# Clustered attention feeding a dense mixture of experts: values' sums on TensorE, scales kept in PSUM, a sign step on ScalarE, three pairs' marks written in place, new ranks in the plan

## The chip, the core and the metric

The kernel runs on one core of a Trainium2 chip. The metric is the device time of one execution in microseconds (us), as the median of several runs. Engines are named as in the profile: PE is TensorE's matmul, PEld its weight load, DVE is VectorE, ACT is ScalarE, POOL is GpSimd, and SP is the queue that issues the DMAs.

## The reference, cut to what matters

```python
def _attn_ref(q, k, v, centroids):                  # q, k, v: (4, 8, 768, 64)
    scale = 1.0 / np.sqrt(D)
    q_assign = np.argmax(np.einsum('bhsd,hcd->bhsc', q_n, c_n), axis=-1)   # 16 clusters
    k_assign = np.argmax(np.einsum('bhsd,hcd->bhsc', k_n, c_n), axis=-1)
    mask = q_assign[:, :, :, None] == k_assign[:, :, None, :]
    scores = np.where(mask, scale * np.matmul(q, k.transpose(0, 1, 3, 2)), -1000000000.0)
    scores = scores - np.max(scores, axis=-1, keepdims=True)
    attn = np.exp(scores)
    attn = attn / (np.sum(attn, axis=-1, keepdims=True) + 1e-09)
    return np.matmul(attn, v)

def _moe_ref(x, w_gate, w1, w2):                    # x: (3072, 512), 8 experts of 1024
    P = np.exp(logits - logits.max())               # logits = x @ w_gate
    ...                                             # 8 rounds: P scaled by its row sums, then its column sums
    for e in range(E):
        out += P[:, e:e + 1] * (np.maximum(x @ w1[e], 0.0) @ w2[e])
```

A query whose cluster has no key at all gets the plain mean of the values: all its scores are equal.

## The kernel before

The program has two stages, each laid out by a planner that is part of the kernel. The first is the attention of 32 heads, in 16 pairs; the second, which starts on PE some 496 us into the execution, is the mixture of experts. Only the attention stage is touched.

**A pair of heads.** `load_pair` brings a pair's q and k in. `scale_pair` takes their sums of squares on ACT (L633), adds them up over the partitions with a product with ones (L639), and works two powers of two out of them on DVE (L642 to L652). `split_pair` writes each operand as a half-precision part and a rest (ACT L666, DVE L668). The parts are transposed: for the first `EARLY` pairs by PE and a copy (`turn`, L698 and L700), for the others by a DMA (L682). `assign_pair` finds the cluster of every row (PE L739 and L750, five DVE steps L756 to L766, PE L778) and puts the clusters as marks into extra rows of the operands `X`: for pair 0 straight out of PSUM (DVE L788, ACT L791), for every other pair by way of a tile `ot` (ACT L802) and four DMAs (L810).

**A head.** `max_chunk` computes scores of 512 columns on PE (L834) and takes their row maximum on DVE (L838), nine chunks a head. `max_rows` turns the maxima into two more rows of the operand (L881, L883, L892). `exp_chunk` computes the scores again with the maxima taken off (PE L930 and L931), takes the exponential on ACT (L937) and adds it up on POOL (L959). `values` multiplies with v on PE in full precision (L995), three times a pair; `norm` divides.

**A group of four heads.** `load_group` loads v and prepares the mean of the values for rows without keys. On DVE two reductions add the six blocks of v (L593, two heads each), one product with ones adds the partitions up (PE L597), a DVE step scales and masks it (`ms`, L600), ACT rounds it (`mh`, L604), and DVE multiplies that with a sign (`mh2`, L608) and adds the rest (`ve`, L611). There are eight groups.

**What sets the order.** Each step is a generator that yields the engine and an estimated duration, and the planner takes the step that can start first, with small rank numbers first among those close together. Instructions then run on each engine in the planned order. Buffers are handed out by `Tokens`: `t_x` stands for the two PSUM tiles named `misc_ps`, which the scales, the clusters, the rows, the group sums and the norms all share. A generator that waits for one gets it by its rank. `"DVE*"` and `POOL` in the plan stand for steps that the planner doesn't lay beside each other.

Of the kernel before, what the change touches and what calls it, by code (L numbers as in the profile page):

```python
# [42 lines left out]
class Tokens:  # L43


    def __init__(self, n):
        self.times, self.waiters = [0.0] * n, []

    def put(self, plan):
        self.times.append(plan.now.time + plan.LATENCY)  # L50
        if self.waiters:
            w = min(self.waiters, key=lambda w: w.key)
            self.waiters.remove(w)
            w.time = max(w.time, self.times.pop())
            plan.resumed.append(w)


class Process:
    def __init__(self, gen, key, time):
        self.gen, self.key, self.time, self.options, self.value, self.engine = gen, key, time, (), None, None  # L60


class Planner:
# [36 lines left out]
    def advance(self, w):  # L100

        while True:
            self.now = w
            try:
                r = w.gen.send(w.value)
            except StopIteration:
                return
            w.value = None
            if isinstance(r, float):
                w.time += r  # L110
            elif isinstance(r, Event):
                if r.time is None:
                    r.waiters.append(w)
                    return
                w.time = max(w.time, r.time)
            elif isinstance(r, Tokens):
                if not r.times:
                    r.waiters.append(w)
                    return
                r.times.sort()  # L120
                w.time = max(w.time, r.times.pop(0))
            else:
# [7 lines left out]
    def run(self):  # L130
        while True:
            while self.resumed:
                self.resumed.sort(key=lambda w: w.key)
                self.advance(self.resumed.pop(0))
# [3 lines left out]
            for i, w in enumerate(self.ready):  # L138
                for o in w.options:
                    engine = o[0].rstrip("*/:")  # L140
                    start = max(w.time + self.latency(w.engine, engine), self.free.get(engine, 0.0))
                    if len(o) == 4:
                        start = max(start, self.loaded + o[2])
                    if o[0] in self.PORT:
                        start = max(start, self.port)
                    if engine == "PE" and o[0][2:] != self.mode:
                        start += 0.1
                    steps.append((start, start + (o[2] if len(o) == 3 else 0.0), w.key, i, w, o, engine))
            first = min(steps, key=lambda x: x[1:4])
# [23 lines left out]
def attn_moe_kernel(  # L173
# [176 lines left out]
    with ExitStack() as actx:  # L350
# [68 lines left out]
        assert 8 * C == P  # L419
        om_scale = const.tile([P, 1], F32, name="om_scale")  # L420
        om_bias = const.tile([P, 1], F32, name="om_bias")
        for h in range(2):
            for t, one, other in ((om_scale, MARK, MARK), (om_bias, 0.0, -MARK)):
                nc.vector.memset(t[4 * h * C : (4 * h + 2) * C, :], one)
                nc.vector.memset(t[(4 * h + 2) * C : 4 * (h + 1) * C, :], other)

# [48 lines left out]

        EARLY = 2
        KEYS = dict(load=-20, split0=-98.0, split1=-72.5, split2=-33.5, assign=-49.0, place=-50.0, chain=-47.5, ones=-49, turn=-40, max=-27, rows=-38.0, exp=0, values=13.5, out=12.0, batch=27.0, group=-30.0, vsplit=-17.0, vsum=-10, group0=-18.5, inputs=8, first=1000)
# [67 lines left out]
        ev = Events()  # L545
        t_x, t_s, t_m, t_v = Tokens(2), Tokens(2), Tokens(2), Tokens(1)
        t_nat, t_sc, t_pe, t_nh, t_vn = Tokens(2), Tokens(1), Tokens(PB), Tokens(6), Tokens(2)
# [21 lines left out]
        def load_group(n):  # L569
            b, g = n // H, n % H // G  # L570
            hs = slice(g * G, (g + 1) * G)
            if True:
                yield ev["x", 0, 1, "k"]
            if n >= G:
                yield ev["e", 0]
            yield t_vn
            t = groups[(b, g)] = {}
            yield SP, 0.625
            vn = vals.tile([P, G, NT, D], F32, name="vn")
            nc.sync.dma_start(  # L580
                out=vn.rearrange("p h t d -> p h (t d)"), in_=v[b, hs].rearrange("h (p t) d -> p h (t d)", t=NT)
            )
            yield plan.copied(3.2) - plan.now.time

            plan.now.key = urgency("vsum", n)
            yield t_mean
            vsum = None
            for i in range(2):
                yield DVE, 0.9
                if i == 0:  # L590
                    vsum = nat.tile([P, G, D], F32, name="vsum", bufs=1)
                hh = slice(i * G // 2, (i + 1) * G // 2)
                nc.vector.tensor_reduce(out=vsum[:, hh], in_=vn[:, hh].rearrange("p h t d -> p h d t"), axis=AX, op=ALU.add)  # L593
            yield t_x
            yield PE, 0.64, 0.107, 0.213
            ps = misc_tile()
            nc.tensor.matmul(ps[:, 0 : G * D], ones, vsum.rearrange("p h d -> p (h d)"), start=True, stop=True)  # L597
            yield DVE, 0.4
            ms = sm.tile([4, G * D], F32, name="ms", bufs=1)
            nc.vector.tensor_tensor(out=ms, in0=ps[0:4, 0 : G * D], in1=halves.rearrange("p h d -> p (h d)"), op=ALU.mult)  # L600
            t_x.put(plan)
            yield ACT, 0.4
            mh = sm.tile([4, G * D], F32R, name="mh", bufs=1)
            nc.scalar.copy(mh, ms)  # L604
            yield ev["cleared"]
            yield "DVE*", 0.45
            mh2 = sm.tile([4, G * D], F32, name="mh2", bufs=1)
            nc.vector.tensor_scalar(out=mh2, in0=mh.bitcast(F32), scalar1=sgn4, scalar2=None, op0=ALU.mult)  # L608
            yield "DVE*", 0.4
            ve = ves[n // G % 2]  # L610
            nc.vector.scalar_tensor_tensor(  # L611
                out=ve[0:4].rearrange("p h d -> p (h d)"), in0=ms, scalar=odd, in1=mh2, op0=ALU.mult, op1=ALU.add
            )
            t_mean.put(plan)
            t.update(vn=vn, ve=ve)
            ev["group", b, g].set(plan)
# [7 lines left out]
        def scale_pair(p):  # L624
# [14 lines left out]
            nc.tensor.matmul(ps[:, 0:2], ones, ss, start=True, stop=True)  # L639
            yield DVE, 0.16  # L640
            g = sm.tile([P, 2], F32, name="sg")
            nc.vector.tensor_scalar(out=g, in0=ps[:, 0:2], scalar1=32.0, scalar2=None, op0=ALU.max)  # L642
            t_x.put(plan)
            yield DVE, 0.6
            nc.vector.tensor_scalar(
# [77 lines left out]
        def assign_pair(p):  # L723
# [55 lines left out]
            plan.now.key = urgency("ones", 2 * p)  # L779
            if p == 0:  # L780
                for x in range(2):
                    for h in range(2):
                        for j, w in enumerate("qk"):
# [5 lines left out]
                            else:  # L789
                                yield ACT, 0.48  # L790
                                nc.scalar.activation(to, psb[rows, 0:HS], AF.Identity, scale=om_scale[rows, :], bias=om_bias[rows, :])  # L791
                    for w in "qk":
                        ev["x", 0, x, w].set(plan)
                t_x.put(plan)
                t_sc.put(plan)
                return
            for h in range(2):
                yield ACT, 0.369
                if h == 0:
                    ot = nat.tile([4 * C, S], F16, name="ot", bufs=1)  # L800
                rows = slice(h * 4 * C, (h + 1) * 4 * C)
                nc.scalar.activation(  # L802
                    ot[:, h * HS : (h + 1) * HS], psb[rows, 0:HS], AF.Identity, scale=om_scale[rows, :], bias=om_bias[rows, :]
                )
# [14 lines left out]
        def max_chunk(n, c):  # L819
# [12 lines left out]
            for y in range(ni):  # L832
# [3 lines left out]
                )  # L836
            yield DVE, 0.598
            nc.vector.tensor_reduce(  # L838
# [76 lines left out]
        def exp_chunk(n, c):  # L915
# [18 lines left out]
            yield t_pe  # L934
            yield ACT, 0.5
            pe = t["pe", c] = work.tile([P, ni, z - a], F32, name="pe", bufs=PB)
# [33 lines left out]
        def values(p):  # L970
# [12 lines left out]
            av = None  # L983
            for u in range(NCH // 3):
                for c in range(3 * u, 3 * u + 3):
                    for x in range(2):
                        yield ev["p", n + x, c]
                yield "PE:", 2.8, 0.107, 0.43
                if u == 0:
                    av = ps_v.tile([P, 1024], F32, name="av_ps")  # L990
                for c in range(3 * u, 3 * u + 3):
                    i0, ni, a, z = CHUNKS[c]
# [922 lines left out]
```

## Time and profile before

| | us |
|---|---|
| median of 3 runs | 2298.12 |
| lowest and highest | 2297.12, 2299.38 |
| the profiled execution | 2296.4 |
| its span, first to last instruction | 2294.5 |
| first product of the second stage on PE | 496 |

The profile is of one execution. For each engine it gives the busy time, for each group of instructions the count and mean duration, and what ended the idle time before them. A view named the chain of waits follows the work that ended last back from the last instruction, from each step to what released it; a piece of it is time that nothing else covered, by that reading. PE's records overlap one another because matmuls are pipelined, so a PE that is busy all the time by its records is not at its peak.

### The profile page before, as it was taken

To read this page: it belongs to the slowest core of one execution; us is meant where nothing else is said; L and a number is where in the kernel's file an instruction comes from. 1 tells how busy PE (TensorE), PEld (TensorE's weight loads), DVE (VectorE), ACT (ScalarE), POOL (GpSimd) and SP (SyncE) were. 2 spreads that over 40 slices of the span, in tenths; PEclk is the share of its full clock that TensorE was granted. 3 is DMA by queue.
4 is the path that set the end of the run, shared out by engine and by line. 5 is a ranking of instruction groups with operands and counts; after the bars stand their busy time and mean duration, and the time that the engine had idled before them with its cause. 6 is when DMAs were issued, how large, how long until landed. Compare 5 with 4: busy or idle time off the path is not lost.

```text
span 2294.5 us, 43172 instructions
## 1 busy us (share of the span) xinstructions
PE 2204.4 (96%) x16218; PEld 1531.3 (67%) x16218; DVE 1886.6 (82%) x3627; ACT 1199.4 (52%) x2318; POOL 1379.0 (60%) x1361
## 2 busy tenths in 40 slices
PE   5899999988989999999999999999999999999998
PEld 2344444445767777777777777777777777777777
DVE  7888988869977987788779877987897789777776
ACT  6577766666555545454535453545454444545432
POOL 5477777979755756464737473747465655556431
PEclk7899999999999999999999999999999999999999
DMA  4556543434522524163426232523343253414242
GB/s 121 125 128 168 133 115 102 134 123 157 194 90 74 180 79 141 58 189 88 142 63 199 70 115 86 170 78 107 122 136 112 72 164 95 134 49 135 61 138 78
DMA packets 176235, 271.00 MB, mean 118 GB/s; under 512 B 59429, under 2 KB 108825, under 8 KB 175513
## 3 DMA queue, kind: packets, MB, share of 16 engines
q1 hardware_dynamic: 176024, 268.24, 39.2%
q8 instruction: 127, 2.08, 0.4%
q14 instruction: 84, 0.68, 0.1%
HBM read 225.82 MB, written 23.69 MB: 109 GB/s over the span
## 4 chain that ended last, share of the span: by engine, by line
PE 82%; DVE 10%; ACT 2%; issue 2%; DMA 2%; POOL 1%; SPq 0%; DVEq 0%; ACTq 0%; POOLq 0%
PE a_ps L1604 21%; PE a_ps L1788 14%; PE ac_ps L1788 12%; PE c_ps L1788 11%; PE c_ps L1604 10%; PE b_ps L1604 5%; PE av_ps L995 3%; DVE mrt L838 3%; PE exp_ps L930 2%; PE max_ps L834 2%; PE exp_ps L931 1%; ACT pe L937 1%; DVE k L668 1%; POOL psum L959 1%; DVE xT L1090 0%
## 5 line engine op out<-in xcount | busy, mean ns | idle before, releaser
L1788 PEld LDWEIGHTS <-h 128*128 128x128 f16 x8064 | 790.1, 98 | 193.3 <-issue 8.1
L1604 PEld LDWEIGHTS <-wa 128*128 128x128 f16 x5376 | 526.6, 98 | 272.7 <-issue 14.5
L1644 POOL TENSOR_TENSOR h<-s,h 128x384 f16<-128x384 f32 x127 | 125.1, 985 | 540.0 <-ACT h L1642 522.9
L1633 ACT ACTIVATE h<-c 128x384 f16<-128x384 f32 x384 | 200.5, 522 | 437.2 <-DVE c L1627 435.7
L1788 PE MATMUL a_ps<-wb,h 128*128 128x256 f16 x3072 | 377.2, 273 | 0.7 <-DVE acc L1828 0.6
L1788 PE MATMUL ac_ps<-wb,h 128*128 128x256 f16 x2688 | 366.6, 273 | 1.4 <-DVE acc L1824 1.4
L1788 PE MATMUL c_ps<-wb,h 128*128 128x256 f16 x2304 | 285.1, 274 | 4.0 <-DVE acc L1824 2.8
L1828 DVE SCALAR_TENSOR_TENSOR acc<-a_ps,gates,acc 128x256 f32<-128x256 f32 x460 | 215.2, 479 | 89.4 <-PE a_ps L1788 86.8
L959 POOL TENSOR_TENSOR psum<-psum,pe 128x256 f32<-128x256 f32 (+1 forms) x240 | 249.5, 1066 | 44.1 <-ACT pe L937 41.2
L1644 POOL TENSOR_TENSOR h<-c,h 128x384 f16<-128x384 f32 x252 | 249.9, 1004 | 23.9 <-ACT h L1642 22.7
L1635 DVE SCALAR_TENSOR_TENSOR h<-c,h 128x384 f16<-128x384 f32 x384 | 254.7, 666 | 6.9 <-ACT h L1633 6.7
L937 ACT ACTIVATE pe<-exp_ps,escs 128x512 f32<-128x512 f32 x288 | 189.8, 683 | 58.2 <-PE exp_ps L931 52.0
L1828 DVE SCALAR_TENSOR_TENSOR acc<-ac_ps,gates,acc 128x256 f32<-128x256 f32 x402 | 192.3, 478 | 33.5 <-PE ac_ps L1788 31.3
L838 DVE TENSOR_REDUCE mrt<-max_ps 128x1 f32<-128x512 f32 (+1 forms) x288 | 189.3, 681 | 36.3 <-PE max_ps L834 34.6
L1828 DVE SCALAR_TENSOR_TENSOR acc<-c_ps,gates,acc 128x256 f32<-128x256 f32 x344 | 155.8, 477 | 74.8 <-PE c_ps L1788 74.3
L1624 ACT ACTIVATE c<-a_ps 128x384 f32<-128x384 f32 x256 | 125.1, 489 | 161.3 <-PE a_ps L1604 159.9
L1642 ACT CAST h<-c 128x384 f16<-128x384 f32 x256 | 128.3, 509 | 83.0 <-DVE c L1718 82.8
L1644 POOL TENSOR_TENSOR h<-h,h 128x384 f16<-128x384 f32 x124 | 139.9, 1128 | 36.0 <-PE c_ps L1788 23.9
L930 PE MATMUL exp_ps<-T 128*128 128x512 f16 (+1 forms) x384 | 125.4, 339 | 9.5 <-ACT pe L937 8.9
L834 PE MATMUL max_ps<-X 96*128 96x256 f16 (+1 forms) x384 | 110.0, 344 | 24.6 <-DVE mrt L838 20.6
L995 PE MATMUL av_ps<-pe,vn 128*64 128x512 f32 (+1 forms) x768 | 133.1, 491 | 0.0
L931 PE MATMUL exp_ps<-X 98*128 98x512 f16 (+1 forms) x384 | 125.5, 339 | 0.9 <-ACT X L865 0.9
(497 smaller groups left out, 3710.7 us busy)
## 6 DMA issues: line engine op xcount, KB each, us to landing
raw<-in_moe_w SPq DMA_DIRECT2D x120, 512.0 KB
qn<-in_q SPq DMA_DIRECT2D x16, 384.0 KB
kn<-in_k SPq DMA_DIRECT2D x16, 384.0 KB
vn<-in_v SPq DMA_DIRECT2D x8, 768.0 KB
xd<-xT SPq DMA_DIRECT2D x4, 1536.0 KB
xqB<-xd SPq DMA_DIRECT2D x16, 384.0 KB
out<-acc SPq DMA_DIRECT2D x16, 384.0 KB
X<-T SPq DMA_DIRECT2D x60, 96.0 KB
```

The lines of the kernel that those rows point to most:

```text
L834: nc.tensor.matmul(ps[:, y * (z - a) : (y + 1) * (z - a)], t["qa"][0:96, i * P : (i + 1) * P], t["k2"][0:96, a:z], start=True, stop=True)
L838: nc.vector.tensor_reduce(out=t["mr"][:, i0 : i0 + ni, ni - 1], in_=ps.rearrange("p (x c) -> p x c", x=ni), axis=AX, op=ALU.max)
L930: nc.tensor.matmul(o, t["k1"][:, ki], t["q1"][:, a:z], start=True, stop=False)
L937: nc.scalar.activation(pe, ps.rearrange("p (x c) -> p x c", x=ni), AF.Exp, scale=pairs[p]["exp"])
L959: (nc.gpsimd if w == POOL else nc.vector).tensor_tensor(out=st[:, a:z], in0=old[a], in1=part, op=ALU.add)
L995: nc.tensor.matmul(av[o, a:z], vn[:, i, :], heads[t]["pe", c][:, i - i0], start=(i == 0), stop=False, skip_group_check=True)
L1604: nc.tensor.matmul(ps[:, 0:HB], wt[:, w_, a, c, :], xv[:, x_, c, :], start=(n in (0, 1, 5) and s_ == 0), stop=(s_ == len(steps) - 1), skip ...
L1633: nc.scalar.activation(t[:, 0], c, AF.Relu)
L1635: nc.vector.scalar_tensor_tensor(out=t[:, 1], in0=c, scalar=0.0, in1=t[:, 0], op0=ALU.max, op1=ALU.subtract)
L1644: by(w).tensor_tensor(out=t[:, 1], in0=c, in1=t[:, 0], op=ALU.subtract)
L1788: nc.tensor.matmul(view(m, i), t[:, a_, i * P : (i + 1) * P], w[:, b_, x, :], start=(opens and n == 0 and i in (0, 2)), stop=(n == 5), ski ...
L1828: nc.vector.scalar_tensor_tensor(out=to, in0=src, scalar=gate[b, e][:, ti : ti + 1], in1=to, op0=ALU.mult, op1=ALU.add)
```

## The change

- **Group sums.** The two DVE reductions are gone; six products of ones with the six blocks of v accumulate in one PSUM tile. The planner's estimate for this step on PE goes from 0.64 to 0.85.
- **Sign step.** ACT writes `mh` already multiplied with the sign (`scale=sgn4`), and the DVE step of `mh2` is gone.
- **Scales.** The four intermediate steps on DVE work in place in the PSUM tile that the product left, and the tile is given back after the fifth instead of after the first.
- **Three early pairs.** `EARLY` is 3 instead of 2, and the first three pairs' marks are written straight from PSUM (DVE and ACT), as pair 0's were. A constant `MARK` replaces the tile `om_scale`.
- **Ranks.** Holding a `t_x` token lifts a generator's rank by 30 until it gives the token back. Two estimates grow (0.598 to 0.66, 0.5 to 0.6). `VU` is 3, which is what stood there.

```diff
-    def __init__(self, n):
-        self.times, self.waiters = [0.0] * n, []
+    def __init__(self, n, lift=0.0):
+        self.times, self.waiters, self.lift = [0.0] * n, [], lift
     def put(self, plan):
+        plan.now.lift -= self.lift
...
-            w = min(self.waiters, key=lambda w: w.key)
+            w = min(self.waiters, key=lambda w: w.key - w.lift)
...
+            w.lift += self.lift
...
-                    steps.append((start, start + (o[2] if len(o) == 3 else 0.0), w.key, i, w, o, engine))
+                    steps.append((start, start + (o[2] if len(o) == 3 else 0.0), w.key - w.lift, i, w, o, engine))
...
-        EARLY = 2
+        EARLY, LIFT, VU = 3, 30.0, 3
...
-        t_x, t_s, t_m, t_v = Tokens(2), Tokens(2), Tokens(2), Tokens(1)
+        t_x, t_s, t_m, t_v = Tokens(2, LIFT), Tokens(2), Tokens(2), Tokens(1)
...
             yield t_mean
-            vsum = None
-            for i in range(2):
-                yield DVE, 0.9
...
-                nc.vector.tensor_reduce(out=vsum[:, hh], in_=vn[:, hh].rearrange("p h t d -> p h d t"), axis=AX, op=ALU.add)
             yield t_x
-            yield PE, 0.64, 0.107, 0.213
+            yield PE, 0.85, 0.107, 0.12
             ps = misc_tile()
-            nc.tensor.matmul(ps[:, 0 : G * D], ones, vsum.rearrange("p h d -> p (h d)"), start=True, stop=True)
+            for i in range(NT):
+                nc.tensor.matmul(ps[:, 0 : G * D], ones, vn[:, :, i, :], start=(i == 0), stop=(i == NT - 1))
...
-            nc.scalar.copy(mh, ms)
+            nc.scalar.activation(mh, ms, AF.Copy, scale=sgn4)
             yield ev["cleared"]
-            yield "DVE*", 0.45
-            mh2 = sm.tile([4, G * D], F32, name="mh2", bufs=1)
-            nc.vector.tensor_scalar(out=mh2, in0=mh.bitcast(F32), scalar1=sgn4, scalar2=None, op0=ALU.mult)
...
-            yield DVE, 0.16
-            g = sm.tile([P, 2], F32, name="sg")
-            nc.vector.tensor_scalar(out=g, in0=ps[:, 0:2], scalar1=32.0, scalar2=None, op0=ALU.max)
-            t_x.put(plan)
-            yield DVE, 0.6
+            yield DVE, 0.8
+            g = ps[:, 0:2]
+            nc.vector.tensor_scalar(out=g, in0=g, scalar1=32.0, scalar2=None, op0=ALU.max)
...
             nc.vector.tensor_scalar(out=es, in0=g[:, 0:1], scalar1=g[:, 1:2], scalar2=SCALE, op0=ALU.mult, op1=ALU.mult)
+            t_x.put(plan)
...
-            if p == 0:
+            if p < EARLY:
...
-                                nc.scalar.activation(to, psb[rows, 0:HS], AF.Identity, scale=om_scale[rows, :], bias=om_bias[rows, :])
+                                nc.scalar.activation(to, psb[rows, 0:HS], AF.Identity, scale=MARK, bias=om_bias[rows, :])
```

The plan of the whole attention stage comes out differently. Two places follow.

PE, right after the first head's rows (`av_ps`) are transposed; `T_185` and `X_186` are head 0's operands, `X_188` head 1's. Before:

```order
L863 MATMUL av_ps<-ident,mr_547 6x128
L930 LDWEIGHTS T_185
L930 MATMUL exp_ps<-T_185 128x512
L931 LDWEIGHTS X_186
L931 MATMUL exp_ps<-X_186 128x512
```

And now:

```order
L855 MATMUL av_ps<-ident,mr_532 6x128
L593 MATMUL misc_ps<-vn,ones 128x256 x6
L826 LDWEIGHTS X_188
L826 MATMUL max_ps<-X_188 128x512
L922 LDWEIGHTS T_185
L922 MATMUL exp_ps<-T_185 128x512
```

The first group's six products, and scores of head 1 for its maxima, now stand ahead of the first scores for an exponential; the group's one product stood some seventy rows further down before.

DVE, where the scales of pair 2 are worked out. Before:

```order
L642 TENSOR_SCALAR sg<-misc_ps 128x2
L758 TENSOR_TENSOR misc_ps<-misc_ps,mx 128x384
L668 SCALAR_TENSOR_TENSOR q_467<-qn,sqk,q_467 128x12x64
L645 TENSOR_SCALAR sg<-sg 128x2
L648 TENSOR_SCALAR sg<-sg 128x2
L650 RECIPROCAL sqk<-sg 128x2
L652 TENSOR_SCALAR escs<-sg 128x1
```

And now:

```order
L596 TENSOR_TENSOR ms<-misc_ps,halves 4x256
L830 TENSOR_REDUCE mrt_236<-max_ps 128x1
L635 TENSOR_SCALAR misc_ps<-misc_ps 128x2
L636 TENSOR_SCALAR misc_ps<-misc_ps 128x2
L639 TENSOR_SCALAR misc_ps<-misc_ps 128x2
L641 RECIPROCAL sqk<-misc_ps 128x2
L643 TENSOR_SCALAR escs<-misc_ps 128x1
```

The five steps now follow one another, all with `misc_ps` as their source, and the group's `ms` stands ahead of them.

## Rows read from the trace of the kernel before

**Rows 1.** The profile page's first line.

```profile
span 2294.5 us, 43172 instructions
```

**Rows 2.** Busy time by stretch, all engines; the first line names the columns.

```profile
core 0: us, PE busy (x) PEld busy (x) DVE busy (x) ACT busy (x) POOL busy (x), PEclk, DMA share, GB/s
...
40.00:45.00 5.00, 4.26 (x14) 1.80 (x13) 5.00 (x9) 4.47 (x8) 1.99 (x2) 0.50 0.21 42
...
30.00:100.00 70.00, 53.03 (x287) 24.79 (x287) 59.22 (x117) 41.54 (x76) 26.90 (x29) 0.79 0.47 107
100.00:300.00 200.00, 186.76 (x1224) 91.86 (x1225) 180.50 (x332) 145.39 (x271) 149.94 (x163) 0.99 0.57 141
300.00:430.00 130.00, 123.38 (x802) 60.43 (x800) 112.86 (x206) 81.01 (x146) 101.19 (x104) 0.97 0.37 106
430.00:496.00 66.00, 60.72 (x339) 26.43 (x334) 40.67 (x62) 44.67 (x77) 48.45 (x48) 0.97 0.38 125
...
560.00:2294.00 1734.00, 1716.63 (x13158) 1287.46 (x13156) 1417.24 (x2752) 826.81 (x1647) 971.48 (x924) 1.00 0.37 114
```

**Rows 3.** Who waited for whom, 0 to 496 us: us, times, longest.

```profile
DVE mrt L838 <- PE max_ps L834: 34.6, 32, 4.5
...
ACT mt L881 <- PE misc_ps L876: 23.3, 14, 3.2
...
PE max_ps L834 <- DVE mrt L838: 20.6, 29, 3.3
ACT q L666 <- DVE sqk L650: 19.7, 11, 2.9
```

**Rows 4.** Chain of waits, 0 to 500 us, pieces: start, us, what.

```profile
7.26 0.56 DVE sg L645
7.85 0.68 DVE sg L648
...
49.46 0.45 PE misc_ps L597 x2
...
64.38 1.41 DVE vsum L593
...
75.82 0.34 DVE mh L608
...
308.00 0.61 DVE sg L645
308.63 0.66 DVE sg L648
...
310.76 0.07 DVE mh L608
...
364.11 0.45 PE misc_ps L597 x2
...
405.94 1.73 DVE vsum L593 x2
```

**Rows 5.** Instructions of single lines: duration ns min/median/max, first and last start.

```profile
L593 DVE TENSOR_REDUCE vsum<-vn x16: 1464/1493/1532, 44.6 to 407.3; 128x128 f32<-128x768 f32 x16
L642 DVE TENSOR_SCALAR sg<-misc_ps x16: 134/151/160, 7.1 to 307.6; 128x2 f32<-128x2 f32 x16
L648 DVE TENSOR_SCALAR sg<-sg x16: 169/651/1193, 7.8 to 308.6; 128x2 f32<-128x2 f32 x16
```

**Rows 6.** In order of time, DVE and POOL near 98 us: start, us.

```profile
98.55 1.18 DVE L648 TENSOR_SCALAR sg<-sg 128x2 f32<-128x2 f32 x1
...
98.44 1.26 POOL L959 TENSOR_TENSOR psum<-pe 128x512 f32<-128x512 f32 x1
```

**Rows 7.** Transposes of a pair by PE (chain), marks by DVE and ACT.

```profile
16.11 1.29 PE exp_ps L698 x12
...
L788 DVE TENSOR_SCALAR X<-misc_ps,keep x4: 408/412/416, 24.7 to 29.2; 32x384 f16<-32x384 f16 x4
```

More of the change, by code (lines that the diff above doesn't have):

```diff
@@ L60, in __init__ @@
         self.gen, self.key, self.time, self.options, self.value, self.engine = gen, key, time, (), None, None
+        self.lift = 0.0
 class Planner:
@@ L121, in advance @@
                 w.time = max(w.time, r.times.pop(0))
+                w.lift += r.lift
             else:
@@ L132, in run @@
             while self.resumed:
-                self.resumed.sort(key=lambda w: w.key)
+                self.resumed.sort(key=lambda w: w.key - w.lift)
                 self.advance(self.resumed.pop(0))
@@ L419, in attn_moe_kernel @@
         assert 8 * C == P
-        om_scale = const.tile([P, 1], F32, name="om_scale")
         om_bias = const.tile([P, 1], F32, name="om_bias")
         for h in range(2):
-            for t, one, other in ((om_scale, MARK, MARK), (om_bias, 0.0, -MARK)):
-                nc.vector.memset(t[4 * h * C : (4 * h + 2) * C, :], one)
-                nc.vector.memset(t[(4 * h + 2) * C : 4 * (h + 1) * C, :], other)
+            nc.vector.memset(om_bias[4 * h * C : (4 * h + 2) * C, :], 0.0)
+            nc.vector.memset(om_bias[(4 * h + 2) * C : 4 * (h + 1) * C, :], -MARK)
         keep = const.tile([P, 1], F32, name="keep")
@@ L586, in load_group @@
             yield t_mean
-            vsum = None
-            for i in range(2):
-                yield DVE, 0.9
-                if i == 0:
-                    vsum = nat.tile([P, G, D], F32, name="vsum", bufs=1)
-                hh = slice(i * G // 2, (i + 1) * G // 2)
-                nc.vector.tensor_reduce(out=vsum[:, hh], in_=vn[:, hh].rearrange("p h t d -> p h d t"), axis=AX, op=ALU.add)
             yield t_x
-            yield PE, 0.64, 0.107, 0.213
+            yield PE, 0.85, 0.107, 0.12
             ps = misc_tile()
-            nc.tensor.matmul(ps[:, 0 : G * D], ones, vsum.rearrange("p h d -> p (h d)"), start=True, stop=True)
+            for i in range(NT):
+                nc.tensor.matmul(ps[:, 0 : G * D], ones, vn[:, :, i, :], start=(i == 0), stop=(i == NT - 1))
             yield DVE, 0.4
@@ L601, in load_group @@
             t_x.put(plan)
-            yield ACT, 0.4
+            yield ACT, 0.45
             mh = sm.tile([4, G * D], F32R, name="mh", bufs=1)
-            nc.scalar.copy(mh, ms)
+            nc.scalar.activation(mh, ms, AF.Copy, scale=sgn4)
             yield ev["cleared"]
-            yield "DVE*", 0.45
-            mh2 = sm.tile([4, G * D], F32, name="mh2", bufs=1)
-            nc.vector.tensor_scalar(out=mh2, in0=mh.bitcast(F32), scalar1=sgn4, scalar2=None, op0=ALU.mult)
             yield "DVE*", 0.4
@@ L611, in load_group @@
             nc.vector.scalar_tensor_tensor(
-                out=ve[0:4].rearrange("p h d -> p (h d)"), in0=ms, scalar=odd, in1=mh2, op0=ALU.mult, op1=ALU.add
+                out=ve[0:4].rearrange("p h d -> p (h d)"), in0=ms, scalar=odd, in1=mh.bitcast(F32), op0=ALU.mult, op1=ALU.add
             )
@@ L790, in assign_pair @@
                                 yield ACT, 0.48
-                                nc.scalar.activation(to, psb[rows, 0:HS], AF.Identity, scale=om_scale[rows, :], bias=om_bias[rows, :])
+                                nc.scalar.activation(to, psb[rows, 0:HS], AF.Identity, scale=MARK, bias=om_bias[rows, :])
                     for w in "qk":
-                        ev["x", 0, x, w].set(plan)
+                        ev["x", p, x, w].set(plan)
                 t_x.put(plan)
@@ L802, in assign_pair @@
                 nc.scalar.activation(
-                    ot[:, h * HS : (h + 1) * HS], psb[rows, 0:HS], AF.Identity, scale=om_scale[rows, :], bias=om_bias[rows, :]
+                    ot[:, h * HS : (h + 1) * HS], psb[rows, 0:HS], AF.Identity, scale=MARK, bias=om_bias[rows, :]
                 )
@@ L836, in max_chunk @@
                 )
-            yield DVE, 0.598
+            yield DVE, 0.66
             nc.vector.tensor_reduce(
@@ L934, in exp_chunk @@
             yield t_pe
-            yield ACT, 0.5
+            yield ACT, 0.6
             pe = t["pe", c] = work.tile([P, ni, z - a], F32, name="pe", bufs=PB)
@@ L983, in values @@
             av = None
-            for u in range(NCH // 3):
-                for c in range(3 * u, 3 * u + 3):
+            for u in range(NCH // VU):
+                for c in range(VU * u, VU * u + VU):
                     for x in range(2):
                         yield ev["p", n + x, c]
-                yield "PE:", 2.8, 0.107, 0.43
+                yield "PE:", 0.93 * VU, 0.107, 0.43
                 if u == 0:
                     av = ps_v.tile([P, 1024], F32, name="av_ps")
-                for c in range(3 * u, 3 * u + 3):
+                for c in range(VU * u, VU * u + VU):
                     i0, ni, a, z = CHUNKS[c]
```

## The prediction

> **What bounds the kernel now.** I read the windows by stretch first. From 560 us to the end PE is busy for 1716.6 of 1734 us at full clock [rows 2]: the second stage is PE's, the change does not touch a line of it, and it begins when the attention ends. So what the attention gains or loses is handed on, one for one, to the end of a span of 2294.5 us [rows 1]. The whole question is the attention, 0 to 496 us.
>
> In it the reader should see three stretches [rows 2]. From 100 to 300 us DVE is busy for 180.5 of 200 us and PE for 186.8: both are near their limit, and PE's share is overstated because its records overlap. From 300 to 430 us DVE falls to 112.9 of 130 and PE stays at 123.4. From 430 us only exponentials, value products and sums are left, and DVE has 25 of 66 us free. Neither engine alone is the bound: PE waited 20.6 us for DVE's maxima and DVE 34.6 us for PE's scores [rows 3]. ACT waited another 19.7 us for the fifth scale step L650 [rows 3]. A microsecond taken off DVE is therefore worth something, but not a whole one, and a microsecond put on PE costs in the same way. The view that weighs this is the chain of waits, so I price each removed step by its pieces there, and not by its busy time.
>
> **Part by part.**
>
> *Group sums, removed side.* Sixteen reductions of 1.493 us, 23.9 us of DVE [rows 5]. On the chain they have six pieces (one of them two instructions long), from the one at 64.38 us to the one at 405.94 us, 6.5 us together [rows 4]. I take 6.5. The ends are 0, if PE's next product was right behind each, and 23.9.
>
> *Group sums, added side.* One product takes PE 0.45 us on the chain [rows 4], so six take 2.7, and each of eight groups adds 2.25 us to PE: 18 us. Before, three of the eight products lay on the chain, from 49.46 to 364.11 us [rows 4]. I take three again: +6.8. The low end is 0. [...] Behind these products PE's in-order queue holds scores and value products, and ACT and POOL wait for those.
>
> *Scales.* The steps L645 and L648 have 12 and 13 pieces on the chain, from 7.26 to 308.63 us, together 13.1 us [rows 4]. L648 handles two numbers per partition; it takes 0.169 us at best, 0.651 at the median and 1.193 at worst [rows 5]. What the difference is can be read near 98 us: it starts at 98.55 us while POOL's sum that began at 98.44 us is running, takes 1.18 us, and ends with it [rows 6]. The step that reads the PSUM tile, L642, never took over 0.160 us in sixteen times [rows 5], and after the change the other steps read PSUM as well. With its median of 0.151 us the 25 pieces shrink to 3.8 us: −9.3. The trace has no step of this size that also writes PSUM, so the ends are 0 (they stay as slow as they are) and −9.3. I take −9.3 since L642 is the nearest row in every other respect. [...]
>
> The price of this part is the tile. It is now held through four more steps of some 0.17 us, 0.7 us longer in each of 16 pairs, 11 us in all. Only two `misc_ps` tiles exist, and the rows of the next head wait in line for one: ACT waited 23.3 us for products into that tile at L876 [rows 3]. The lift of ranks works against that.
>
> *Sign step.* L608's four pieces on the chain, from 75.82 to 310.76 us, are 2.2 us [rows 4]. ACT's rounding step stays one instruction of the same size. I take −2.2, between 0 and that.
>
> *Three early pairs.* Pair 2's 24 transposes move to PE, at twelve in 1.29 us [rows 7] 2.6 us. Pairs 1 and 2 need eight more mark steps of 0.412 us on DVE [rows 7], 3.3 us, and as many on ACT; SP loses four transposes and eight small transfers. From 30 to 100 us ACT has 28 of 70 us free, PE 17 and DVE 11 [rows 2], so much of the 5.9 us hides; without that cover it costs 5.9. What it may bring is that marks come without a trip through DMA; DVE's longest wait for scores was 4.5 us [rows 3], and I let that be the gain's end. I take +1.0, near the middle.
>
> *Ranks.* They decide the order of everything and cannot be read from a duration. As an estimate, if the lift takes a fifth off the 23.3 us of waiting for `misc_ps` it gives 4.7 us; if the tiles' 11 us of longer holding fall on the path for a third, it costs 3.7. I take 0.
>
> Sum: −6.5 + 6.8 − 9.3 − 2.2 + 1.0 = −10.2 us. The profiled execution took 2296.4 us, 1.9 more than its span [rows 1] and 1.7 less than the median of 2298.1. So 2286.2 for it, and 2287.9, about 2288 us, for the median.
>
> **The rivals.**
>
> *PE becomes the bound (slower).* The six products are the dearest form of work that PE has, and they add 18 us to an engine that is already busy for 186.8 of 200 us from 100 to 300 us [rows 2]. If all eight lie on the path, the first of them at half the clock, they cost 20.7; and if two thirds of the 18 us of savings (6.5 + 9.3 + 2.2) were only covering a wait for PE, 6 are left: 20.7 − 6 + 1 = +15.7, 2314 us. It decides from the point at which half of the savings are gone and more than four of the eight groups are on the path (9 against 4 × 2.25). Against it: five of eight were not on the chain before, and DVE and ACT waited for each other's results often enough to leave gaps. For it: DVE waited longer for PE than PE for DVE [rows 3].
>
> *The savings run into waits that stood right behind (no change).* Half of the 18 is given back: −9 + 6.8 + 1 = −1.2, 2297 us. For it speaks the same pair of rows.
>
> *The scales do not get quicker (no change).* If steps that also write PSUM still wait for POOL, the 9.3 falls away: −0.9, 2297 us. Against it: L642 never waited.
>
> *The relief spreads (more gain).* DVE loses 23.9 us of reductions and the slow scales, early marks let the heads of pairs 1 and 2 start sooner, and the lift frees `misc_ps`: −18 + 0 − 4.5 − 4.7 = −27, 2271 us; with three groups' products on the path still −20, 2278. For it: DVE's 180.5 of 200 us. Against: PE is as full there.
>
> **How the numbers follow.** My forecast has 0.50, the two rivals of no change 0.17 and 0.05, the slower one 0.15 and the greater gain 0.13. A measurement of this kernel can tell about 0.2%, 4.6 us, from no change. The forecast and the greater gain lie beyond that on the fast side, less a little of the forecast's near edge: faster 0.62. The two of no change and that edge with a part of the slower rival's mild form: same 0.22. Slower 0.16. The range goes from 2274, between the greater gain's two prices, to 2303, a third of the way into the slower rival (+5 us), and leaves out the ends of both.
>
> **What would show it.** In the profile of the changed kernel: L648's successor (L639) at about 0.15 us with no value over 0.3; twelve records (two per product) per group at L593 that take 2.6 to 2.7 us; DVE's busy time from 100 to 300 us well below 180 of 200; the first product of the second stage on PE near 486 us instead of 496, and everything after it moved by the same amount. I am wrong if DVE gets freer and that product does not come sooner: then PE's waits for DVE have turned into waits for PE itself, and the pieces of L593 on the chain will say how many groups were paid for. I am wrong in another way if ACT's waits at L876's successor grow, which would be the longer-held tile.

## The result, and the profile after

The changed kernel takes 2318.5 us (median of 4 runs, 2314.7 to 2319.8) where the kernel before took 2297.9 in the same comparison: a ratio of 1.0084, 95% interval 1.007 to 1.0098. It is 0.84% slower, and the forecast of 2288 us was wrong in its sign; 2318.5 lies 15 us above the range. The profiled execution took 2314.7 us, with a span of 2312.9, 18.4 more than before [rows 1].

Where the time went is read from the second stage, which the change does not touch. The row of its weight loads gives first and last start:

```profile
L1596 PEld LDWEIGHTS <-wa x5376: 95/98/181, 511.2 to 2287.7; 128*128 128x128 f16 x200
```

It begins at 511.2 us instead of 496: 15.2 of the 18.4 us were lost in the attention. The other 3 came in the opening of the second stage: its products that started at 617.7 us before start 15.1 us later now, those of 678.4 us 17.6 and those of 766.8 us 18.5, and from there on the distance stays. From 575 us on PE is busy for 1719.5 of 1737 us, before for 1716.6 of 1734 from 560 us on [rows 2].

The windows of the changed kernel (busy time by engine, then PE's granted clock) answer to [rows 2]:

```profile
core 0: us, PE busy (x) PEld busy (x) DVE busy (x) ACT busy (x) POOL busy (x), PEclk, DMA share, GB/s
...
30.00:100.00 70.00, 62.29 (x392) 33.49 (x385) 59.64 (x128) 49.51 (x91) 34.04 (x37) 0.90 0.38 93
100.00:300.00 200.00, 187.53 (x1201) 94.86 (x1199) 156.92 (x311) 136.33 (x258) 146.93 (x152) 1.00 0.57 143
300.00:430.00 130.00, 121.82 (x745) 59.48 (x745) 95.12 (x182) 79.28 (x142) 102.07 (x105) 0.99 0.41 124
430.00:511.00 81.00, 74.00 (x414) 32.74 (x411) 48.12 (x78) 47.96 (x85) 54.02 (x51) 0.96 0.20 70
575.00:2312.00 1737.00, 1719.51 (x13161) 1288.83 (x13159) 1420.60 (x2753) 826.79 (x1647) 969.29 (x924) 1.00 0.37 114
```

DVE was relieved as planned: 156.9 of 200 us from 100 to 300 us instead of 180.5, 95.1 of 130 instead of 112.9. The second stage did not come sooner for it. ACT does less in the same stretch (136.3 instead of 145.4): its exponentials fall behind. Counted by ACT's exponentials in order of time, nine a head, the first head ends 9.8 us later than before (60.0 instead of 50.2 us), the third 10.8 us sooner (92.1 instead of 102.9) and the eighth 4.9 us sooner (167.4 instead of 172.3). At the eleventh the lead is gone; the eighteenth ends at 312.8 instead of 306.7, the last at 508.1 instead of 492.8. An early lead of 11 us is real, and it is lost again from 110 us on.

Who waited for whom, 0 to 512 us of the changed kernel (us, times, longest), beside [rows 3]:

```profile
DVE mrt L830 <- PE max_ps L826: 37.9, 30, 7.6
ACT mt L873 <- PE misc_ps L868: 33.0, 17, 2.7
...
ACT sc L1032 <- PE misc_ps L1025: 23.4, 11, 4.4
...
PEld misc_ps L1025 <- POOL psum L951: 17.3, 17, 3.1
...
PE max_ps L826 <- DVE mrt L830: 14.8, 28, 1.3
```

PE waits less for DVE (14.8 us instead of 20.6), and ACT's wait for the scale step that writes `sqk` (L650 before; it is the fourth of the five), 19.7 us before, is down to 1.0. ACT's wait for the rows' products (`mt`) has grown from 23.3 to 33.0. Two further waits stand there: PE's weight loads for the norms wait for POOL's sums, and ACT waits 23.4 us for those products (`sc`; 3.3 us before).

The scale steps and the group sums, single lines of the changed kernel (duration ns min/median/max, first and last start), answer to [rows 5]:

```profile
L593 PE MATMUL misc_ps<-vn,ones x96: 377/379/631, 37.5 to 413.5; 128*128 128x256 f32 x96
...
L635 DVE TENSOR_SCALAR misc_ps<-misc_ps x16: 152/168/169, 7.4 to 306.7; 128x2 f32<-128x2 f32 x16
...
L639 DVE TENSOR_SCALAR misc_ps<-misc_ps x16: 168/168/168, 7.8 to 307.1; 128x2 f32<-128x2 f32 x16
```

L639 does what L648 did, in PSUM: 0.168 us sixteen times, against a median of 0.651 and a worst of 1.193. (Three steps work in place in the tile, L635, L636 and L639; the fourth and fifth only read it.) That POOL no longer holds them up can be read from single instructions. Before, eleven of the sixteen L648 began while POOL was in an instruction, and ten of these ended within 0.03 us behind it. Now nine of the sixteen L639 began so, and each took its 0.168 us and ended before POOL's instruction did; one of them (start, us):

```profile
278.29 2.51 POOL L951 TENSOR_TENSOR psum<-psum,pe 128x512 f32<-128x512 f32 x2
...
279.90 0.17 DVE L639 TENSOR_SCALAR misc_ps<-misc_ps 128x2 f32<-128x2 f32 x1
```

The step costs no more in PSUM at this size: 0.168 us there, 0.169 at best in SBUF [rows 5].

A group's twelve records, in order of time on PE (start, us), the first two groups:

```profile
37.49 4.52 PE L593 MATMUL misc_ps<-vn,ones 128*128 128x256 f32 x12
60.59 2.75 PE L593 MATMUL misc_ps<-vn,ones 128*128 128x256 f32 x12
```

The prediction gave a group 2.7 us, and its slower rival had the first one at half the clock. A group takes 2.75, and the first one 4.52 at a granted clock of 0.59 from 37 to 42 us: its first nine records start 0.427 us apart and its last three 0.216, as those of the other groups do. With 0.38 us for most records and 0.216 from one start to the next, the records overlap. On the chain of waits from 0 to 512 us all eight groups have a piece, 22.5 us together (start, us, what; the first three):

```profile
37.69 4.33 PE misc_ps L593 x12
...
60.75 2.61 PE misc_ps L593 x12
...
121.92 2.61 PE misc_ps L593 x12
```

### The profile page after: what moved, and what is told of

Its sections match the earlier page's. It is cut to its first block, busy times and chain, and to the rows that moved or that the text cites. A ratio compares the mean times of both kernels' runs of the same rounds, so it can differ in the third digit from the quotient of the medians.

```text
span 2312.9 us, 43335 instructions
## 1 busy us (share of the span) xinstructions
PE 2227.1 (96%) x16322; PEld 1548.4 (67%) x16322; DVE 1855.6 (80%) x3607; ACT 1200.7 (52%) x2325; POOL 1386.2 (60%) x1362
## 4 chain that ended last, share of the span: by engine, by line
PE 85%; DVE 6%; ACT 3%; POOL 3%; issue 2%; DMA 2%; SPq 0%; DVEq 0%; ACTq 0%; POOLq 0%
PE a_ps L1596 21%; PE a_ps L1780 14%; PE ac_ps L1780 12%; PE c_ps L1780 10%; PE c_ps L1596 10%; PE b_ps L1596 5%; PE av_ps L987 3%; POOL psum L951 2%; PE exp_ps L922 2%; PE max_ps L826 2%; PE exp_ps L923 1%; DVE mrt L830 1%; ACT pe L929 1%; PE misc_ps L593 1%; PE misc_ps L1025 1%
## 5 line engine op out<-in xcount | busy, mean ns | idle before, releaser
L1596 PEld LDWEIGHTS <-wa 128*128 128x128 f16 x5376 | 526.6, 98 | 277.7 <-issue 19.1
L951 POOL TENSOR_TENSOR psum<-psum,pe 128x256 f32<-128x256 f32 (+1 forms) x240 | 254.7, 1089 | 48.9 <-ACT pe L929 45.5
L922 PE MATMUL exp_ps<-T 128*128 128x512 f16 (+1 forms) x384 | 122.0, 330 | 10.6 <-ACT pe L929 9.5
L826 PE MATMUL max_ps<-X 96*128 96x256 f16 (+1 forms) x384 | 108.5, 335 | 18.4 <-DVE mrt L830 14.8
```

What stands on the lines that cost most here:

```text
L826: nc.tensor.matmul(ps[:, y * (z - a) : (y + 1) * (z - a)], t["qa"][0:96, i * P : (i + 1) * P], t["k2"][0:96, a:z], start=True, stop=True)
L922: nc.tensor.matmul(o, t["k1"][:, ki], t["q1"][:, a:z], start=True, stop=False)
L951: (nc.gpsimd if w == POOL else nc.vector).tensor_tensor(out=st[:, a:z], in0=old[a], in1=part, op=ALU.add)
L1596: nc.tensor.matmul(ps[:, 0:HB], wt[:, w_, a, c, :], xv[:, x_, c, :], start=(n in (0, 1, 5) and s_ == 0), stop=(s_ == len(steps) - 1), skip ...
```

## The experiments

All are timed in rounds beside the kernel before on the same chip. A ratio is to those runs, with its 95% interval; a difference of two ratios is turned into microseconds by 2296 us, about what the kernel before takes on these chips. The intervals make such a difference uncertain by 0.0013 to 0.0024, 3 to 6 us.

### What do the six products cost?

**One product instead of six.** The changed kernel with one product per group, so that five of the six blocks of v are left out of the mean of the values. No estimate is touched, so that every other instruction stands where it stood.

```diff
-            for i in range(NT):
-                nc.tensor.matmul(ps[:, 0 : G * D], ones, vn[:, :, i, :], start=(i == 0), stop=(i == NT - 1))
+            nc.tensor.matmul(ps[:, 0 : G * D], ones, vn[:, :, 0, :], start=True, stop=True)
```

> The changed kernel with only the first of each group's six products, so the mean of the values is wrong in this run (five of six blocks of v are left out of it); the plan and every other instruction are the same. First theory, the products' own time on PE: six groups have 15.6 us on the chain of waits after the change, five sixths of that go, so about 2305 us. Second theory, the lifted ranks put the norms' products ahead of POOL's sums and PE waits there: the products only fill PE's gaps, at most 4 us go, 2314 to 2319 us.

2294.2 us, ratio 1.0001 (0.9991 to 1.001). Against the changed kernel's 1.0084 the forty products left out are worth 0.0083, 19 us. By their length on PE (the products of a group start 0.432 us apart at full clock, granted 1.00 from 121 to 126 us) five come to 2.16 us, eight times that is 17.3, and the first group has 1.8 more at the low clock: 19.1. So the groups are paid for nearly in full, not three of eight. The second stage begins 15.8 us sooner (495.4 instead of 511.2 us); the rest comes in its opening. That is more than either theory expected: the first counted the six groups that lie on the chain from 100 us on, and all eight do from its start.

**The same without the lift.** `LIFT = 0`, one product; the order is that of the run without the lift, below.

> The changed kernel with a lift of 0 and only the first of each group's six products (five of six blocks of v are left out of the mean of the values); the plan is that of the run without lift, row for row. Five products of 0.44 us in eight groups are 17.6 us of PE. If they lie on the path with or without the lift, this run takes 2278 to 2282 us, against 2297.4 with all six. If it was the lift's order that put them on the path, it takes 2292 us or more.

2281.4 us, 0.993 (0.9913 to 0.9946), against 1.0014 with six products: 0.0084, 19 us again; the second stage begins 14.2 us sooner (483.7 instead of 497.9). The price does not hang on the lift, nor on PE's clock: with the products left out the mean granted clock of the profiled execution went up in the first pair of runs (0.989 to 0.994) and down in the second (0.992 to 0.989).

**The sums back on DVE.** The changed kernel with the old reductions and the single product (and its old estimate, so the order changes too).

```diff
+            for i in range(2):
+                yield DVE, 0.9
+                ...
+                nc.vector.tensor_reduce(out=vsum[:, hh], in_=vn[:, hh].rearrange("p h t d -> p h d t"), axis=AX, op=ALU.add)
...
-            yield PE, 0.85, 0.107, 0.12
+            yield PE, 0.64, 0.107, 0.213
```

> The changed kernel with the group sums as before: two reductions on DVE and one product. First theory (products): PE loses 18 us of work and DVE has room for 24 us, 2300 to 2306 us. Second theory (lift): PE's waits for POOL at the norms stay near 25 us and the time stays at 2313 us or above.

2301.9 us, 1.0034 (1.0021 to 1.0048): 0.005, 11 us better than the changed kernel. The reductions that come back cost 0.0033 against one product with none, 7.6 us, in another order.

### What does the lift cost?

**No lift.** One number: `LIFT` from 30.0 to 0.0.

> The changed kernel with a lift of 0, so the ranks are as they were before the change; the plan is worked out anew. Second theory (lift): PE's waits for POOL's sums at the norms fall from 24.7 us to the 5.4 of before, and the time to 2298 to 2302 us. First theory (products): the waits may fall, but the time stays at 2312 to 2320 us.

2297.4 us, 1.0014 (1.0005 to 1.0023): the lift costs the changed kernel 0.007, 16 us.

**The lift alone.** The kernel before with the planner's lift and `t_x = Tokens(2, 30.0)`, and nothing else of the change.

> The kernel before with the lift of ranks by 30 alone. If the lift is a loss of its own, as the run without it says (2297.4 against some 2313.5 us on one chip), this run takes 2306 to 2312 us, and the waits of the norms for POOL's sums grow from 5.4 us to some 25. If the lift only hurts together with the six products, it takes 2292 to 2297 us.

2315.8 us, 1.0084 (1.0065 to 1.0103): 19 us, in another kernel. Two more pairs of these runs differ in the lift alone: with one product 1.0001 against 0.993 (0.0071, 16 us), with the sums on DVE 1.0034 against 0.993 (0.0104, 24 us). The prediction had put the ranks at 0, between −4.7 and +3.7.

### The other parts

**Scales and sign alone.** The kernel before with the scale steps in PSUM and the sign step on ACT.

```diff
-            g = sm.tile([P, 2], F32, name="sg")
+            g = ps[:, 0:2]
...
-            nc.scalar.copy(mh, ms)
+            nc.scalar.activation(mh, ms, AF.Copy, scale=sgn4)
```

> The kernel before with the scales in PSUM and the sign step on ScalarE alone. By the chain of waits of before 11.5 us go: 2283 us. If the tile held through five steps costs as much as the shorter steps give, 2292 to 2296 us. If the longer-held tile is the cause of the loss, above 2300 us.

2287.1 us, 0.9956 (0.9942 to 0.9971): a gain of 0.0044, 10 us, where the prediction had 9.3 + 2.2. The second and third scale step have 20 pieces on this run's chain, 3.6 us together, and ACT's wait for `sqk` is 7.2 us instead of 19.7.

**Two early pairs.** The changed kernel with `EARLY = 2` and only pair 0's marks copied directly.

> The changed kernel with pair 2 again transposed by DMA and pairs 1 and 2 marked by way of the tile and its transfers. The changed kernel's exponentials were 11 us ahead at the third head and 13 at the fifth. If that lead is the third early pair's and lasts, this run takes 2328 to 2332 us; if the steady part swallows any lead, it takes 2316 to 2322 us.

2317.3 us, 1.0100 (1.0085 to 1.0115). That is 0.0016, some 4 us more than the changed kernel, but the intervals overlap: a gain from the third early pair is not shown, and its early lead does not last.

**Neither lift nor products.** The changed kernel with `LIFT = 0` and the sums on DVE: what is left of the change is the scales, the sign, the early pairs and a few estimates.

> The changed kernel with a lift of 0 and the group sums on DVE as before; left of the change are the scales in PSUM, the sign step, the three early pairs and the estimates. If these parts are worth what the chain of waits gave for them before (9.3 and 2.2 us), and DVE's reductions cost their 6.5 again, this run takes 2281 to 2286 us. If relief of DVE is worth nothing in this stage, it takes 2293 to 2297 us.

2281.1 us, 0.993 (0.9915 to 0.9945). It beats both kernels, by 16 us the one before and by more than 30 the changed one.

**The true length in the plan.** No lift, six products, and 2.7 us instead of 0.85 as the planner's estimate for them.

> The changed kernel with a lift of 0 and an estimate of 2.7 us for the six products, in place of 0.85. If the products cost so much because the planner did not know their length, it can lay them beside other work: 2284 to 2290 us. If their time on TensorE is the price whatever the plan, 2295 to 2299 us.

2294.1 us, 1.0000 (0.999 to 1.0009): 0.0014 better than with the false estimate, about 3 us, at the edge of what these intervals tell. By this one order, hardly any of the products' 19 us comes from the planner's not knowing their length.

**Another order, nothing else.** The kernel before with one estimate changed from 0.598 to 0.60, which reorders the stage from early on; no work changes.

> The kernel before with one estimate changed from 0.598 to 0.600, which reorders the plan from row 548 of PE on and changes no work. It measures what a reordering alone is worth: within 5 us of before if plans are alike, 10 us or more if single plans scatter so much that the other runs' differences mean little.

2302.6 us, 1.0035 (1.0022 to 1.0048): 8 us from a reshuffle that means nothing. A single difference of that size between two orders proves no mechanism; the lift's 16 to 24 us are at least twice as much, and are found in each of four pairs of kernels.

### By which wait does the lift lose its time?

The first theory was that the norms are to blame because their own rank is lifted. Two kernels split the lift of the kernel before.

```diff
@@ in norm, lift for all others
         yield t_x
+            plan.now.lift -= 30.0
@@ in norm, lift for norms alone
         yield t_x
+            plan.now.lift += 30.0
```

> The kernel before with the lift for every holder of a misc tile but the norms. Theory, norms: lifted, the norms' products come on TensorE before POOL's last sums are done, and their copy (sc) then blocks ScalarE's queue with exponentials behind it (23.2 us of such waits with the lift, 3.3 without). Then this run takes 2294 to 2300 us and those waits are near 3. Rival, any lift spoils the plan (scales, clusters and rows too): 2308 us or more.

> The kernel before with the lift for the norms alone. Theory, norms: 2310 to 2318 us, with some 20 us of waits of the copy sc for the norms' products. Rival: the loss needs the other holders, 2296 to 2303 us.

Lift for all but the norms: 2298.1 us, 1.0017 (1.0007 to 1.0026). Lift for the norms alone: 2296.6 us, 1.0009 (1.0 to 1.0018). Neither loses the 19 us, nor do both together. That theory fell in its simple form.

What the full lift does can be counted in PE's order. Each pair's scores for the exponentials are 24 products of L922 (L930 before) on PE, and its norm can only be computed when all of them have become exponentials on ACT and have been added up, most of them on POOL. In the kernel before, the norm of a pair mostly stands 3 such products behind the pair's last one, so that the next pair's scores cover the wait; with the lift it stands 1 behind. The wait is read from the norm's own line:

| kernel | products between (median of 16 pairs) | PE idle until POOL's sums, us | ratio |
|---|---|---|---|
| before | 3 | 5.4 | 1 |
| lift for all but norms | 3 | 7.6 | 1.0017 |
| lift for norms alone | 3 | 0.8 | 1.0009 |
| changed, no lift | 4 | 8.0 | 1.0014 |
| changed, no lift, one product | 4 | 8.1 | 0.993 |
| changed, no lift, sums on DVE | 3 | 7.4 | 0.993 |
| lift alone | 1 | 15.0 | 1.0084 |
| changed, sums on DVE | 1 | 23.7 | 1.0034 |
| changed, one product | 1 | 25.1 | 1.0001 |
| changed | 1 | 24.7 | 1.0084 |

The ratios differ by the other parts too; the lift's price is read from kernels that differ in it alone. Only the two halves together bring the norms forward. A likely reason, which no run shows, is that a lifted norm gets no further if the tiles that it needs come back no sooner. The norms' line in the kernel before and in the changed one (what its engine waited for, who waited for it):

```profile
L1033 PE MATMUL misc_ps<-psum,ones x128: 482/486/782, 77.1 to 495.6; 128*32 128x384 f32 x128
...
  POOL psum L959: 5.4, 3
...
  ACT sc L1040: 3.3, 3
...
L1025 PE MATMUL misc_ps<-psum,ones x128: 483/510/849, 82.8 to 510.4; 128*32 128x384 f32 x128
...
  POOL psum L951: 24.7, 22
...
  ACT sc L1032: 23.4, 11
```

One such place on the chain of waits of the changed kernel (start, us, what):

```profile
390.27 1.95 POOL psum L951 x2
392.22 0.19 POOL flags L903
392.41 1.24 POOL psum L951
393.64 0.69 POOL sums L1400
394.33 0.07 issue
394.40 3.51 POOL sums L1400 x3
397.92 5.21 POOL psum L951 x5
403.12 0.04 issue
403.17 2.17 PE misc_ps L1025 x6
405.34 0.54 PE exp_ps L922
405.88 0.43 PE exp_ps L923
```

POOL is in the middle of other sums (L1400), PE stands at the norm until 403.17, and behind it in PE's queue are the scores of the next head; ACT's `sc` stands likewise ahead of exponentials. Added up over the chain from 100 us to the end of the attention, POOL's psum has 42.6 us in 14 pieces, in the kernel before 11.5 in 5.

Three kernels take that wait away and leave every instruction in its place: the norms' products read the constant ones instead of POOL's sums, so the division by the sums is left out of them.

```diff
-                    ps[...], ones[:, 0:Q], heads[n + g // 2]["sum"][:, ...], start=True, stop=True
+                    ps[...], ones[:, 0:Q], ones.unsqueeze(1).broadcast_to([P, HS // P, P]), start=True, stop=True
```

> The changed kernel, row for row, with the same single operand changed: the norms' products read the constant ones instead of POOL's sums, and the division by the sums is left out (it is by a constant). Theory A (the lift's loss is the norms' wait for POOL's sums): it falls by 12 to 18 us, to 2301 to 2307 us. Theory B (the order as a whole): 2312 us or above.

> The kernel before, row for row, with the same single operand changed: the norms' products read the constant ones instead of POOL's sums, and the division by the sums is left out (it is by a constant). This is the measure for lift_no_sums_wait: what the waits for the sums cost without the lift, where ACT waited only 3.3 us for the norms' products. Both theories: between 2292 and 2298 us. If it falls by 10 us or more, the sums' wait costs as much without the lift and says nothing on the lift.

> The kernel before with the lift of 30 for all holders of misc_ps, and every engine's instructions in the same rows as in lift_alone. One operand differs: the norms' products (L1037) read the constant ones instead of POOL's sums, so they no longer wait for POOL, and the division by the sums is left out (it is by a constant). Theory A: the lift's 18 us come from norms that stand early on PE, wait there for POOL's sums, and hold ACT's copy sc and the exponentials queued behind it. Then most of it goes: 2297 to 2302 us, and ACT's wait for the norms' products falls from 23.2 to under 6 us. Theory B: the lift costs by the order as a whole (products of a later head before scores of an earlier one), and the wait for the sums only shows where the engines would be waiting anyway: it stays at 2310 us or above. Between 2303 and 2309 both have a part.

In the changed kernel: 2294.6 us, 1.0002 (0.9993 to 1.0012), a gain of 0.0082, 19 us. The norms' line there, and the second stage's first weight load:

```profile
L1025 PE MATMUL misc_ps<-ones x128: 486/486/511, 82.8 to 492.9; 128*32 128x384 f32 x128
...
  ACT sc L1032: 8.7, 7
...
L1596 PEld LDWEIGHTS <-wa x5376: 95/98/181, 493.8 to 2267.1; 128*128 128x128 f16 x200
```

PE no longer waits for POOL there, ACT's `sc` waits 8.7 us instead of 23.4, and the second stage begins 17.4 us sooner. ACT's wait for the rows' products (L873) is still 34.1 us, so that wait, on which the prediction had watched the longer-held tile, is not what these 19 us went into. A part of the gain may come by way of PE's clock: from 430 to 494 us it is granted 0.95 in the changed kernel and 1.00 without the wait, at most some 3 us (an estimate, 5% of 64 us). In the kernel before, the same edit gives 0.9994 (0.9984 to 1.0003), nothing that can be told from zero. For the changed kernel this settles it: the wait for POOL's sums is worth 19 us, as much as the lift (16) within the intervals. What the wait is worth in the changed kernel without the lift, where it is 8.0 us long, was not measured.

In the kernel with the lift alone the edit gives back only 0.0025, 6 us of 19, at the edge of the intervals: 2307.6 us, 1.0059 (1.0044 to 1.0074), between what the two theories expected. The wait there was smaller too (15.0 us). ACT still waits 15.2 us for the norms' products in it, so they may be early against more than POOL, which is not shown; some 13 us of the lift's price in that kernel stay open.

## Why the prediction was wrong

Following single steps from the kernel before to the changed one, by ratios: scales and sign −0.0044 (−10 us), third early pair and estimates with the sums still on DVE −0.0026 (−6), six products for DVE's sums +0.0084 (+19), the lift +0.007 (+16); together +0.0084, the measured ratio. Each of these steps also reorders the plan, which alone can move some 8 us, and the split hangs on the order of the steps: with the lift taken first it is 24 us for the lift and 11 for the products. Their sum of 35 does not. The products' price is the firmest: five of the six were measured twice in an unchanged order.

- **Group sums, added side: the step that failed first.** "I take three again: +6.8." Measured 19, next to the slower rival's 20.7. That price is eight times 2.25 us and 2.7 more for a first group wholly at half the clock; no run shows the 2.7: the first group took 1.8 us more than the others (4.52 instead of 2.75). The chain of before was asked a question that it cannot answer: it says which of eight products of 0.45 us were on it, but a product six times as long puts itself there. PE was busy for 186.8 of 200 us [rows 2], in order, with the scores of later heads behind each group; 2.25 us more found hardly a gap at any of the eight places. The chain of after does show it: L593 has eight pieces there, 22.5 us, and five sixths of that are 18.8.
- **Group sums, removed side.** −6.5 by pieces of the chain. Between 0 (without the lift: 0.993 with the reductions and one product, 0.993 with one product alone) and 7.6 us (with it). The size was fair, though either pair differs in its order too; the trade of 24 us on DVE for 18 on PE was a loss because PE pays nearly in full and DVE hardly at all.
- **Ranks: the step that failed second.** 0, from −4.7 to +3.7. Measured +16 to +24 within the changed kernel and, alone, +19. The prediction looked only at who waits for a `misc_ps` tile. It did not ask which of the tile's users waits for something else while it stands first in PE's queue: the norm, for POOL's sums.
- **Scales and sign.** −9.3 and −2.2, measured −10 together, in an order of its own. The mechanism was right: none of the three steps in PSUM over 0.169 us in the changed kernel, ACT's wait for `sqk` down from 19.7 to 7.2 us with this part alone. The sum was not quite: the chain of before has L648 in 12 pieces and not 13, one having been counted twice, so it is 11.9 us in 24 pieces instead of 13.1 in 25, and −8.3 instead of −9.3 by the same rule. That is what the run's chain shows (11.9 to 3.6).
- **Three early pairs.** +1.0; the runs have gains of 4 and 6 us, the first within the intervals, the second together with the estimates and a new order, so neither is shown. The lead of 11 us at the third head comes with this part and the scales, and is lost later.
- **The rivals.** The slower one gave 2314 and came nearest. Its price for the products was right (20.7 for 19), and dear they are: 0.432 us for a product of 256 columns, where scores of 256 columns (L922) start 0.11 us apart. Its other half was not: the savings of the scales and the sign did not vanish as cover for a wait for PE, they are there alone (−10 us) and without lift and products (−16 us with the early pairs). What made up for it is the lift, which no rival had as a cost; so that it came so near is luck. Without the lift the kernel is within 0.2% of before.
- **What would show it.** L639 (0.168 us for 0.15), the records of L593 (2.75 us, but for the first group) and DVE's busy time came much as forecast; the second stage's start did not (511.2 instead of 486). The forecast's test for being wrong, DVE freer and that start no sooner, is what happened, and the pieces of L593 say that eight groups were paid for. The other sign came as well, ACT's longer wait for the rows' products (33.0 us instead of 23.3), but 19 us come back in a run in which that wait is as long (34.1).

## What to carry to other kernels

Work that is moved onto an in-order engine which is busy nine tenths of the time (PE, 186.8 of 200 us) costs, here, nearly its whole length (19 us for 19.1); the chain of waits of the old kernel tells what a removal gives, not what a longer instruction in the same place will cost. The chain of the new kernel did, read from its start. Before raising a rank because a buffer is scarce, list what each holder of that buffer waits for: one that waits for a third engine blocks the queue that it was moved ahead in (here PE's, for 24.7 us). And a part of a change that wins can hide in one that loses; here two parts out of five cost 35 us, and the kernel without them is 0.7% faster than the one before.

## What the runs showed of the hardware that was not expected

Small DVE steps that read and also write PSUM (L639) take 0.168 us sixteen times out of sixteen, nine times beside a running POOL instruction, with POOL about as busy as before (146.9 of 200 us); no row of the kernel before had such a step. Nor does every small step in SBUF wait for POOL: before, seven of the sixteen L650, whose tiles are both in SBUF, began beside a running POOL instruction, and none took over 0.167 us. Nothing else was unexpected of the chip itself: what surprised was in the order of the work.
